# First layer's last block by halves: two head groups and the feed-forward in 256-token halves, two tiles per bank, seam transposes by DMA, a new table of settings

## The chip, the cores and the metric

One core of one Trainium2 chip runs the whole program. The metric is device time in microseconds (us) of one launch, lower is better. "The page" below is the page of one profiled execution; its span runs from that execution's first to its last instruction.

## What is computed

Two identical layers over 2048 tokens of width 512, each an attention with 32 heads of 16 and a gated feed-forward of width 1792, both with a layer norm ahead and a residual add behind. Inputs are bf16.

```python
def _A_ref(x, wqkv, wo):                      # H = 32, Dh = 16
    q, k, v = split(x @ wqkv)                 # (B, H, S, Dh) each
    p = softmax(einsum("bhqd,bhkd->bhqk", q, k) * Dh ** -0.5)
    return merge(einsum("bhqk,bhkd->bhqd", p, v)) @ wo
def _B_ref(x, w_gate, w_up, w_down):
    return (gelu(x @ w_gate) * (x @ w_up)) @ w_down
x = A_x
for _ in range(2):
    x = x + _A_ref(_layernorm(x), A_wqkv, A_wo)
    x = x + _B_ref(_layernorm(x), B_w_gate, B_w_up, B_w_down)
return x
```

## The kernel before

Everything stays on chip between the loads and the sixteen output stores. The order of all work is made at build time by a planner at the end of `_build`: it keeps a clock of its own per engine, looks at which pieces of work could start, and emits one at a time, so that each engine gets a fixed list of instructions with semaphore waits. The table `PLAN` gives the planner twenty numbers that change along the program (its key counts the first pass's score tiles planned so far, in fours); they say, among other things, how long a lead the first pass may have, from which lead a copy out of PSUM goes to VectorE and not to ScalarE, and how many small matmuls go at a time.

**Attention** is done per unit: four heads (a head group, eight groups per layer) by one block of query tokens (512; the second layer's last 512 are two blocks of 256). A unit goes through two passes.

- First pass: TensorE multiplies 128 queries by 512 keys of one head into one PSUM bank (L2453), VectorE takes the row maxima of one or two banks at a time (L2468) into PM. GpSimd joins the maxima (L1597 to L1602), VectorE transposes them (L1608), and SyncE's DMA queue writes the negative maximum into a spare row of QT (L1626).
- A tile can be folded: GpSimd subtracts two key blocks (KD, L2039), TensorE multiplies with the difference (L2276), ScalarE takes its relu (L2283), and one VectorE instruction (L2463, with a short read of its accumulator) adds it to the second tile's scores and takes the maximum. That spares VectorE one of two tiles and costs ScalarE one.
- Second pass: TensorE multiplies keys by queries (L2331), ScalarE takes the exponential of one or two banks (L2303) into a slot of SCR, and TensorE multiplies with V (L2356, 17 columns, the last for the sum) into bank 7. `nrm` divides (L1650 on ScalarE, L1656 and L1661 on GpSimd) into ATT.

**Behind a block's last unit** follow the output projection (ATT transposed into ATTT, matmul with WO, residual add into X at L1669 on VectorE, or L1674 on ScalarE and L1676 on GpSimd), a layer norm (statistics on VectorE or GpSimd, XN), its transpose into XNT, and the feed-forward `ffn`. In it a gate matmul fills a bank with one tile of the hidden width, the bank is copied to HT (L1309 VectorE, L1311 ScalarE), five instructions `gate` make the gelu on GpSimd (L1799, L1801, L1803, L1807, L1809) with a tanh on ScalarE (L1805), an up matmul fills another bank, and the product is taken either on VectorE straight from PSUM (L1971) or by a copy on ScalarE (L1977) and a multiplication on GpSimd (L1979). The down matmuls and the residual add close the block. The last block of a layer takes ScalarE's gelu (L1958) in place of `gate`; during it no exponentials are planned. Matmuls of projections and feed-forwards are L1294.

**Transposes** go one of two ways. `transpose_tile`: four 128x128 TensorE transposes into a bank (L1423) and one copy out (L1309, L1311). `transpose_dma`: one DMA transpose issued on SyncE's queue (L1430), SBUF to SBUF. Before the change the DMA way is taken for all blocks except the first layer's last one (its ATT, and XN both of its feed-forward and of the next layer's input), and except the program's end.

**The seam.** The second layer's attention needs keys of all 2048 tokens. So behind the last exponential of the first layer its last block has to run through projection, feed-forward, layer norm and key projection before the second layer's second pass can begin. The planner fills that time with first-pass tiles of six units on the keys that are there. TensorE also gets matmuls on zeros (L2486) where the planned load of the last microseconds is low.

`SPL` and `SPL0` are the numbers of last head groups that go by halves in the last block of the second and of the first layer; `half_of` and `u_half` mark these halves, and a halved block gets two output projections and two feed-forwards.

## Time and profile before

| what | us |
|---|---|
| median of 3 runs (lowest, highest) | 2467.43 (2465.78, 2468.37) |
| the profiled execution's own time | 2465.77 |
| its span | 2464.0 |
| busy in it: TensorE / VectorE / ScalarE / GpSimd | 2394.3 / 2393.6 / 2321.7 / 1271.1 |
| granted TensorE clock | 1.000 |

Busy time counts overlapping instructions of an engine once. The mean of a group counts each instruction from start to end, and neighbours overlap a little, so a mean is more than what an instruction adds to its engine. TensorE's busy time holds the matmuls on zeros.

### The profile page before, as it was taken

Reading aid. Unit: us, or ns where it says so; the run is one execution under the profiler, and the core shown is the slowest. Engines: PE = TensorE matmul, PEld = TensorE weight load, DVE = VectorE, ACT = ScalarE, POOL = GpSimd, SP = SyncE. Lnnn points to the kernel's source line nnn. Section 1 sums busy time; section 2 is a strip of 40 time slices with the busy share of each in tenths; the row PEclk is TensorE's granted clock in tenths of the full one; section 3 lists DMA queues with packets and bytes.
Section 4 is the critical chain, followed back from the end, with each engine's and each line's share of the span. In section 5 each row is a group of like instructions: output and inputs, shape, how many; then the busy total and the mean of one; then the engine's idle time right before and its main releaser. Section 6 shows DMA issues by size and latency. Waiting matters only on the chain.

```text
span 2464.0 us, 69105 instructions
## 1 busy us (share of the span) xinstructions
PE 2394.3 (97%) x29671; PEld 1141.9 (46%) x29671; DVE 2393.6 (97%) x3252; ACT 2321.7 (94%) x3103; POOL 1271.1 (52%) x2168
## 2 busy tenths in 40 slices
PE   8999999999999999999999999999999999999999
PEld 3444444444444444444433555454454444444456
DVE  9999999999999999999999999999999999999995
ACT  7999999999999999999966999999999999999897
POOL 5121137975579645965243211379317781279482
DMA  3110000000000001001000000000000000000000
GB/s 95 49 60 9 4 13 13 2 6 11 15 11 2 9 8 21 4 8 28 4 7 10 5 4 4 13 13 4 10 4 17 7 2 8 13 15 4 18 5 13
DMA packets 62747, 33.64 MB, mean 14 GB/s; under 512 B 44904, under 2 KB 61416, under 8 KB 62440
## 3 DMA queue, kind: packets, MB, share of 16 engines
q1 hardware_dynamic: 62440, 29.22, 4.8%
q8 instruction: 232, 3.80, 0.6%
q14 instruction: 75, 0.61, 0.1%
HBM read 9.70 MB, written 2.10 MB: 5 GB/s over the span
## 4 chain that ended last, share of the span: by engine, by line
DVE 38%; PE 36%; ACT 24%; POOL 1%; issue 1%; DMA 0%; POOLq 0%; ACTq 0%; DVEq 0%; SPq 0%
DVE PM L2468 34%; ACT SCR L2303 22%; PE PS L2453 12%; PE PS L1294 10%; PE PS L2356 8%; PE PS L2331 3%; PE PS L2486 2%; DVE SCR L2463 2%; ACT SCR L2283 1%; DVE HT L1971 1%; DVE HT L1092 0%; PE PS L2276 0%; ACT ACCS L1650 0%; ACT SCR L1805 0%; PE PS L1423 0%
## 5 line engine op out<-in xcount | busy, mean ns | idle before, releaser
L2468 DVE TENSOR_REDUCE PM<-PS 128x1 f32<-128x512 f32 (+1 forms) x2502 | 2162.7, 927 | 34.7 <-PE PS L2331 13.6
L2303 ACT ACTIVATE SCR<-PS 128x1024 bf16<-128x1024 f32 (+1 forms) x2439 | 2012.1, 929 | 67.8 <-PE PS L2331 48.7
L2453 PE MATMUL PS<-KT,QT 32*128 32x512 bf16 x3870 | 1027.3, 384 | 40.2 <-DVE PM L2468 23.2
L2331 PE MATMUL PS<-QT,KT 32*128 32x512 bf16 (+2 forms) x4864 | 920.5, 349 | 3.1 <-ACT SCR L2303 1.8
L2356 PE MATMUL PS<-VP,SCR 128*128 128x51 bf16 (+1 forms) x16384 | 812.3, 187 | 12.8 <-ACT SCR L2303 8.4
L2356 PEld LDWEIGHTS PS<-VP,SCR 128*128 128x128 bf16 x16384 | 576.3, 96 | 507.9 <-issue 426.6
L2453 PEld LDWEIGHTS PS<-KT,QT 32*128 32x128 bf16 x3870 | 245.1, 91 | 506.3 <-DVE PM L2468 301.7
L2486 PE MATMUL PS<-WV,ZER 128*128 128x240 bf16 x2031 | 377.8, 265 | 0.7 <-ACT SCR L2303 0.7
L1656 POOL TENSOR_TENSOR RL<-ACCS,CM 128x16 f32<-128x16 f32 (+2 forms) x66 | 179.6, 2721 | 359.1 <-ACT ACCS L1650 359.0
L2331 PEld LDWEIGHTS PS<-QT,KT 32*128 32x128 bf16 x4864 | 234.1, 91 | 68.8 <-ACT SCR L2303 41.7
L1597 POOL TENSOR_TENSOR PM<-PM 128x32 f32<-128x32 f32 (+2 forms) x76 | 18.5, 243 | 397.0 <-DVE PM L2468 385.7
L2486 PEld LDWEIGHTS PS<-WV,ZER 128*128 128x128 bf16 x2031 | 153.2, 96 | 51.5 <-issue 43.8
L2463 DVE CUSTOM_DVE_ANT_0 SCR<-PS,SCR 128x512 bf16<-128x512 f32 x226 | 145.8, 685 | 2.6 <-PE PS L2453 1.0
L1294 PE MATMUL PS<-WD,HT 128*128 128x512 bf16 x448 | 139.3, 381 | 0.4 <-DVE AO L2020 0.2
L1294 PE MATMUL PS<-XNT,WU 128*128 128x512 bf16 (+2 forms) x560 | 136.1, 338 | 2.3 <-DVE HT L1971 1.0
L2283 ACT ACTIVATE SCR<-PS 128x1024 bf16<-128x1024 f32 (+1 forms) x116 | 120.3, 1042 | 11.3 <-PE PS L2276 10.2
L1294 PE MATMUL PS<-XNT,WG 128*128 128x512 bf16 (+2 forms) x560 | 130.2, 338 | 0.7 <-ACT HT L1311 0.3
L2039 POOL TENSOR_TENSOR KD<-KT 128x512 bf16<-128x512 bf16 x74 | 85.4, 1154 | 86.8 <-PE PS L2276 76.2
L1799 POOL TENSOR_TENSOR SCR<-HT 128x512 bf16<-128x512 bf16 (+1 forms) x98 | 96.0, 980 | 43.0 <-ACT HT L1311 33.7
L1809 POOL TENSOR_TENSOR HT<-HT,SCR 128x512 bf16<-128x512 bf16 (+1 forms) x98 | 106.3, 1085 | 5.0
L1803 POOL TENSOR_TENSOR SCR<-SCR,HT 128x512 bf16<-128x512 bf16 (+1 forms) x98 | 106.2, 1085 | 2.4
L1676 POOL TENSOR_TENSOR X<-X,AO 128x512 f32<-128x512 f32 x42 | 53.2, 1268 | 75.4 <-ACT AO L1674 75.0
(128 smaller groups left out, 1498.3 us busy)
## 6 DMA issues: line engine op xcount, KB each, us to landing
KT<-SG SPq DMA_DIRECT2D x64, 64.0 KB
QT<-SG SPq DMA_DIRECT2D x56, 64.0 KB
QT<-MT SPq DMA_DIRECT2D x216, 1.0 KB
out_dram<-AO SPq DMA_DIRECT2D x16, 128.0 KB, 1.7
WG<-in_B_w_gate_dram SPq DMA_DIRECT2D x4, 448.0 KB, 4.8
WU<-in_B_w_up_dram SPq DMA_DIRECT2D x4, 448.0 KB, 4.9
WD<-in_B_w_down_dram SPq DMA_DIRECT2D x4, 384.0 KB, 4.6
QT<-MT SPq DMA_DIRECT2D x72, 0.5 KB
```

Source lines behind the costliest of these rows:

```text
L1294: ins = e.matmul(out_ap, lhsT=l, rhs=r_, start=(i == 0), stop=(i == n - 1))
L1656: emit("pool", lambda e: e.tensor_tensor(RL[:, s, 0:4 * nq], lsum, CM1[:, 0:4 * nq], op=ALU.pow), r=[("ACCS", s), ("CM1",)], w=[("RL", s)] ...
L1803: emit("pool", lambda e: e.tensor_tensor(u, u, ht, op=ALU.mult), r=ku + kh, w=ku, dur=0.18 + n / 520.0)
L1809: emit("pool", lambda e: e.tensor_tensor(ht, ht, u, op=ALU.mult), r=ku + kh, w=kh, dur=0.18 + n / 520.0)
L2283: emit("act", lambda e: e.activation(PT[:, s0:s0 + cnt, :], PS[:, bk:bk + cnt, :], ACTF.Relu), r=bks, w=[("PT", s0 + d) for d in range(cnt ...
L2303: emit("act", lambda e: e.activation(dst, src, ACTF.Exp, scale=DH ** -0.5), r=[BK[bk + i] for i in range(cnt)], w=[("PT", i) for i in slot ...
L2331: ins = e.matmul(bank(bk)[:, i * n:(i + 1) * n], lhsT=KT[32 * j:32 * j + 32, g, kt * 128:(kt + 1) * 128], rhs=QT[32 * j:32 * j + 32, s, c0 ...
L2356: ins = e.matmul(acc, lhsT=PT[:, slot, i * nh + (qt - q0) * 128:i * nh + (qt - q0 + 1) * 128], rhs=AP(VP, (kt * H + 4 * g + j) * 17, [[NTT ...
L2453: ins = e.matmul(bank(b), lhsT=QT[32 * j:32 * j + 32, s, qt * 128:(qt + 1) * 128], rhs=KT[32 * j:32 * j + 32, g, kb * 512:(kb + 1) * 512], ...
L2463: emit("dve", lambda e, i=i, b=b, sl=sl: e.tensor_tensor_reduce(PT[:, sl, :], bank(b), PT[:, sl, :], 1.0, -3.0e38, ALU.add, ALU.max, po[:, ...
L2468: emit("dve", lambda e: e.tensor_reduce(po, PS[:, bs[0]:bs[0] + cnt, :], axis=AX.X, op=ALU.max), r=bks, w=[("PM", sm) + h[1:] for h in hs] ...
L2486: return e.matmul(PS[:, b, NACC:512], lhsT=ZER[:, :], rhs=WV[:, 0, 0:512 - NACC], start=(b != 7), stop=(b != 7), skip_group_check=True)
```

## The change

Four switches of `_build` change, and the table is new: 566 entries in place of 625, 347 keys in common, one of these with the same numbers.

```diff
-... FAST=1, TG=1, ... SPL0=0, ... HQ=0, TP=1, LAGX=84, G2=0, CAL=0, XD=3, XDT=0.6, XDN=4):
+... FAST=1, TG=1, ... SPL0=2, ... HQ=0, TP=1, LAGX=84, G2=0, CAL=0, XD=15, XDT=0.6, XDN=2, PK=1):
...
-    0: (0.4, 0.35, 0.65, 0.32, 1.0, -0.05, 3, 1, 62, 84, 8, 80, 0.1, 1.5, 10, 10, 1, 4, 11, 84),
...
-                if XD & 1 and not fast and (tts[-1] < 12 or (tag[0] == "mid" and tag[1] == NL - 1)):
+                if XD & 1 and not fast and (XD & 4 or tts[-1] < 12 or (tag[0] == "mid" and tag[1] == NL - 1)):
...
-            dt = XD & 2 and not lastb and (la == NL - 1 or t0 + n < S)
+            dt = XD & 2 and not lastb and (XD & 8 or la == NL - 1 or t0 + n < S)
...
-        def gate(ft, n, due, done, cnt=1):
-            if cnt == 2:
+        def gate(ft, n, due, done, cnt=1, h=None, pk=False):
+            hc = (256 + h * n if h is not None and n <= 128 else h * n if h else 0) if HQ else n if h == 1 else 0
+            if cnt == 2 and not pk:
...
+                u = PT[:, sl, 0:cnt * n].rearrange("p (a b) -> p a b", a=cnt) if pk else PT[:, sl, 0:n]
...
             done = set()
-            for ft in range(NFT if tg else 0):
+            pk = PK and tg and n == 256
+
+            def gemm_p(W, wkey, f0, hk):
...
+                for i in range(2):
+                    if i:
+                        yield ("pe", [], [], NCK * n / 2300.0)
+                    pairs = [(W[:, ck, (f0 + i) * 128:(f0 + i + 1) * 128], XNT[:, ck, t0:t0 + n]) for ck in range(NCK)]
+                    emit_pe(mm_fn(bank(b)[:, i * n:(i + 1) * n], pairs, range(NCK)), NCK, n, r=xk + [(wkey,)], w=[BK[b]])
...
+            for f0 in range(0, NFT if pk else 0, 2):
+                hk = [k for ft in (f0, f0 + 1) for k in ht_keys(ft, h, n)]
+                b = yield from gemm_p(WG, "WG", f0, hk)
+                evac(HV[:, f0:f0 + 2, :], bank(b)[:, 0:2 * n].rearrange("p (a b) -> p a b", a=2), [BK[b]], hk, 2 * n)
+                add(gate(f0, n, due, done, 2, h, True), due)
+            for ft in range(NFT if tg and not pk else 0):
...
+            for f0 in range(0, NFT if pk else 0, 2):
...
+                yield ("cond", lambda f0=f0: f0 in done and f0 + 1 in done)
+                b = yield from gemm_p(WU, "WU", f0, hk)
...
+                if fast or pick() == "dve":
+                    emit("dve", lambda e, src=src, dst=dst: e.tensor_tensor(dst, src, dst, op=ALU.mult),
...
+                    emit("act", lambda e, b=b, o=o: e.activation(AO[:, o, 0:2 * n], bank(b)[:, 0:2 * n], ACTF.Copy),
...
+                    emit("pool", lambda e, dst=dst, o=o: e.tensor_tensor(
...
-            for ft in range(NFT):
+            for ft in range(0 if pk else NFT):
```

With `SPL0=2` the last two of the eight head groups of the first layer's last block are four units of 256 tokens in place of two of 512; the first half's output projection and feed-forward can go ahead of the second half's exponentials. `PK` puts two 256-token tiles of the hidden width into one bank, so that one copy, one gate and one product serve both; it holds for the first half here (the second half, as a layer's last, takes ScalarE's gelu, one tile at a time) and for the second layer's first 256-token block. Bits 4 and 8 of `XD` send the seam's transposes by DMA, twelve 128-token tiles in all. `XDN` is how many units of SyncE's issue time the planner books for a DMA transpose. The shorter table and the new code shift the line numbers: L2468 before is L2455 after, L1971 is L1952, L1977 is L1958, L1294 is L1235, L2331 is L2318, L2453 is L2440, L1430 is L1371.

Three places show how the instructions move. **TensorE around the last exponentials of the first layer.** Before, the last matmuls for exponentials (QT,KT) stand among products with V (VP,SCR) and first-pass tiles (KT,QT):

```order
L2453 MATMUL PS<-KT,QT 128x512 x2
L2331 MATMUL PS<-QT,KT 128x512 x2
L2356 MATMUL PS<-VP,SCR 128x3x17 x3
L2356 MATMUL PS<-VP,SCR 128x51
L2356 MATMUL PS<-VP,SCR 128x2x17
```

After, there are 256-token tiles, and the first half's gate matmuls (WG) stand between them, its first up matmuls (WU) right behind:

```order
L1235 MATMUL PS<-XNT,WG 128x256 x4
L2440 MATMUL PS<-KT,QT 128x512
L1235 MATMUL PS<-XNT,WG 128x256 x4
L2318 MATMUL PS<-QT,KT 128x256 x4
L2343 MATMUL PS<-VP,SCR 128x3x17 x4
L2440 MATMUL PS<-KT,QT 128x512 x2
L2343 MATMUL PS<-VP,SCR 128x3x17 x8
L1235 MATMUL PS<-XNT,WU 128x256 x8
```

All 56 gate matmuls of the first half now stand ahead of the last of those; before, all gate matmuls of that block stood behind.

**SyncE's queue over the seam.** QT<-SG and QT<-ZER fill queries, KT<-SG the keys, QT<-MT the negative maxima. Before:

```order
L1573 DMA QT<-ZER 4x4x128
L1575 DMA QT<-SG 64x512
L1489 DMA KT<-SG 64x512 x14
L1626 DMA QT<-MT 4x2x32 x8
L1626 DMA QT<-MT 4x4x32 x20
```

After:

```order
L1514 DMA QT<-ZER 4x4x128
L1516 DMA QT<-SG 64x512
L1371 DMA_TRANSPOSE ATTT<-ATT 128x4x128 x2
L1430 DMA KT<-SG 64x512 x6
L1371 DMA_TRANSPOSE XNT<-XN 128x4x128 x6
L1430 DMA KT<-SG 64x512 x8
L1567 DMA QT<-MT 4x2x32 x8
L1567 DMA QT<-MT 4x4x32 x20
```

Eight transposes now stand in that stretch of the queue, which had none, and the last eight key moves stand behind six of them.

**The product of the feed-forward in the first layer's third block.** Before, on VectorE, between the first-pass reductions:

```order
L1971 TENSOR_TENSOR HT<-PS,HT 128x512
L2468 TENSOR_REDUCE PM<-PS 128x1
L2468 TENSOR_REDUCE PM<-PS 128x2
L1608 STREAM_TRANSPOSE MT<-MSEL 128x32
L2468 TENSOR_REDUCE PM<-PS 128x1
L1971 TENSOR_TENSOR HT<-PS,HT 128x512
L2468 TENSOR_REDUCE PM<-PS 128x2
```

After, the same products are copies on ScalarE, between the exponentials (L2290), with a multiplication on GpSimd behind each:

```order
L2290 ACTIVATE SCR<-PS 128x1024
L2290 ACTIVATE SCR<-PS 128x512
L1958 ACTIVATE AO<-PS 128x512
L2290 ACTIVATE SCR<-PS 128x1024
L2290 ACTIVATE SCR<-PS 128x512
L1749 ACTIVATE SCR<-SCR 128x512
L1958 ACTIVATE AO<-PS 128x512
```

Over the first layer's first three blocks 25 of 42 products were on VectorE; now 3 are.

More of the change, by code (lines that the diff above doesn't have):

```diff
@@ L1947, in ffn @@
                 if not G2:
[L1948 removed]
+                    add(gate(ft, n, due, done, 1, h), due)
                 elif ft % 2:
[L1950 removed]
+                    add(gate(ft - 1, n, due, done, 2, h), due)
             if not tg:
```

41 lines of the change are left out of this document (31 added, 10 removed), and 1188 rows, old and new, of the table PLAN.

## The prediction

> **What bounds the kernel now.** First the page's busy times, the slices of the span and the chain of waits:
>
> ```profile
> PE 2394.3 (97%) x29671; PEld 1141.9 (46%) x29671; DVE 2393.6 (97%) x3252; ACT 2321.7 (94%) x3103; POOL 1271.1 (52%) x2168
> DVE  9999999999999999999999999999999999999995
> ACT  7999999999999999999966999999999999999897
> POOL 5121137975579645965243211379317781279482
> DVE 38%; PE 36%; ACT 24%; POOL 1%; issue 1%; DMA 0%; POOLq 0%; ACTq 0%; DVEq 0%; SPq 0%
> ```
>
> VectorE is idle for 2464.0 - 2393.6 = 70.4 us, ScalarE for 142.3. TensorE's 97% holds matmuls on zeros, so it is no bound over the whole span. ScalarE has its hole in slices 20 and 21: the seam. GpSimd is loaded in stretches, those of the feed-forwards. So I cut the span at the seam with the view of windows; the cuts are the last exponential of the first layer, the first of the second, and the 768th exponential bank after it (columns: length, then busy us of PE, weight loads, DVE, ACT, POOL):
>
> ```profile
> core 0: us, PE busy (x) PEld busy (x) DVE busy (x) ACT busy (x) POOL busy (x), PEclk, DMA share, GB/s
> 0.00:1224.50 1224.50, 1188.21 (x14405) 556.57 (x14405) 1208.83 (x1662) 1178.11 (x1564) 664.38 (x1165) 1.00 0.07 19
> 1224.50:1337.90 113.40, 108.77 (x596) 37.54 (x595) 107.41 (x195) 68.13 (x97) 49.29 (x100) 1.00 0.04 10
> 1337.90:1709.50 371.60, 365.05 (x5012) 185.65 (x5013) 359.99 (x459) 367.40 (x424) 144.22 (x244) 1.00 0.03 7
> 1709.50:2464.00 754.50, 732.25 (x9660) 362.15 (x9658) 717.40 (x939) 708.05 (x1019) 413.23 (x660) 1.00 0.04 10
> ```
>
> Four stages. **A**, 1224.5 us: VectorE idle 15.7, ScalarE 46.4; VectorE bounds. **B**, the seam, 113.4 us: VectorE idle 6.0, TensorE 4.6, ScalarE 45.3. **C1**, 371.6 us: ScalarE idle 4.2, VectorE 11.6; here ScalarE bounds, since VectorE came out of the seam with a lead. **C2**, 754.5 us: VectorE idle 37.1, ScalarE 46.4, much of it at the end. Shorter windows say how close the two engines can come:
>
> ```profile
> 0.00:44.00 44.00, 37.05 (x262) 18.87 (x262) 38.66 (x74) 33.08 (x51) 30.67 (x51) 1.00 0.44 132
> 44.00:88.00 44.00, 42.70 (x429) 16.73 (x429) 43.63 (x83) 38.42 (x56) 5.26 (x21) 1.00 0.05 13
> 440.00:484.00 44.00, 43.19 (x460) 17.95 (x456) 43.16 (x53) 41.64 (x66) 40.92 (x48) 1.00 0.01 2
> 880.00:924.00 44.00, 42.41 (x580) 21.63 (x575) 43.95 (x63) 43.96 (x50) 12.94 (x36) 1.00 0.03 5
> 2420.00:2464.00 44.00, 40.76 (x659) 28.41 (x659) 18.32 (x53) 28.50 (x56) 4.72 (x13) 1.00 0.06 17
> ```
>
> Where no feed-forward runs (880 to 924) both are full. In a feed-forward (440 to 484) ScalarE has 2.4 us free, VectorE 0.8, and GpSimd is 93% busy. ScalarE's 46.4 us in A are 16.5 at the start (10.9 and 5.6) and some 30 later. The last 44 us idle VectorE for 25.7; that tail has the same instructions after the change, but for two more exponential banks (40 for 38) behind the last first-pass tile, some 1 us.
>
> **Prices.** The group rows of the page give what neighbours overlap:
>
> ```profile
> L2468 DVE TENSOR_REDUCE PM<-PS 128x1 f32<-128x512 f32 (+1 forms) x2502 | 2162.7, 927 | 34.7 <-PE PS L2331 13.6
> L2303 ACT ACTIVATE SCR<-PS 128x1024 bf16<-128x1024 f32 (+1 forms) x2439 | 2012.1, 929 | 67.8 <-PE PS L2331 48.7
> ```
>
> 2502 x 0.927 is 2319.4 us, busy 2162.7: 0.063 us of each reduction lies over its neighbour. On ScalarE it is (2439 x 0.929 - 2012.1) / 2439 = 0.104. The forms apart, by lines:
>
> ```profile
> L2468 DVE TENSOR_REDUCE PM<-PS 128x2 f32<-128x1024 f32 x1142 | 1387.8, 1218 | 22.4 <-PE PS L2331 8.3 <-PE PS L2453 7.2 <-PE PS L2276 0.7
> L2468 DVE TENSOR_REDUCE PM<-PS 128x1 f32<-128x512 f32 x1360 | 914.2, 682 | 12.3 <-PE PS L2331 5.3 <-PE PS L2453 3.3 <-PE PS L2276 0.3
> L2463 DVE CUSTOM_DVE_ANT_0 SCR<-PS,SCR 128x512 bf16<-128x512 f32 x226 | 145.8, 685 | 2.6 <-PE PS L2453 1.0 <-PE PS L2331 0.7
> L2463 DVE DVE_READ_ACCUMULATOR2_ANT PM<- 128x1 f32 x226 | 18.8, 83 | 0.0
> L1971 DVE TENSOR_TENSOR HT<-PS,HT 128x512 bf16<-128x512 f32 x48 | 32.7, 681 | 0.2 <-PE PS L1294 0.2
> L2303 ACT ACTIVATE SCR<-PS 128x1024 bf16<-128x1024 f32 x1657 | 1607.5, 1079 | 52.9 <-PE PS L2331 38.0 <-DVE PM L2468 1.1 <-PE PS L2453 0.3
> L2303 ACT ACTIVATE SCR<-PS 128x512 bf16<-128x512 f32 x782 | 460.9, 611 | 14.9 <-PE PS L2331 10.6
> L2283 ACT ACTIVATE SCR<-PS 128x1024 bf16<-128x1024 f32 x110 | 116.5, 1065 | 11.3 <-PE PS L2276 10.2
> L1977 ACT ACTIVATE AO<-PS 128x512 f32<-128x512 f32 x50 | 30.5, 610 | 5.6 <-PE PS L1294 5.6
> ```
>
> Less the overlap: VectorE reduction of two banks 1.155, of one 0.619, fold 0.622 + 0.083 = 0.705, product 0.618; ScalarE exponential of two banks 0.975, of one 0.507, relu of two 0.961, copy 0.506.
>
> **The change part by part**, each engine's instructions counted in the order before and after and priced so.
>
> *Stage A.* VectorE: 22 products fewer (25 to 3), -13.6; 15 folds fewer, -10.6; 10 two-bank and 7 one-bank reductions more, +15.9; layer-norm statistics and transposes of the second half, +1.7. Sum -6.6. ScalarE: 22 copies for products more, +11.1; 16 one-bank exponentials more and 8 two-bank ones fewer, +0.3; relus 5 two-bank and 5 one-bank fewer, -7.4; some eleven copies and tanhs more, the first half's gate copies among them, +5.5. Sum +9.5. So VectorE would need 1202.2 and ScalarE 1187.6. If VectorE bounds as before, A shortens by 6.6, and ScalarE's idle time falls from 46.4 to 30.3, of which 16.5 are the start: 14 us left over 1130, closer than now but not closer than the window 880 to 924. The other end: ScalarE keeps its 46.4 idle us, and A grows by 9.5. The order keeps folding where VectorE would be late, so the two meet; I take -4.5, near the first end, since VectorE is the fuller engine in every feed-forward window. The two-tile copies and products (128x2x256) have no row; they lie between one copy of 512 (0.506) and two of 256, and I take the former, at most 3 us for all of them.
>
> *Stage B.* VectorE's list in it has 5 reductions, 2 statistics and one product fewer, 118.4 to 113.5 us by the same prices: -4.9. ScalarE -3.9. TensorE: 244 matmuls of 512 columns (two of 256 counted as one) for 280, because the first half's gate matmuls and half of the projection went ahead; no transposes for 12 groups of four; 24 matmuls on zeros more:
>
> ```profile
> 1323.27 2.76 PE L1294 MATMUL PS<-XNT,WK 128*128 128x512 bf16 x12
> 1333.65 0.79 PE L2486 MATMUL PS<-WV,ZER 128*128 128x240 bf16 x6
> 1320.96 0.34 PE PS L1423 x4
> 1321.32 0.61 ACT XNT L1311
> L1430 SPq DMA_TRANSPOSE XNT<-XN x38: 1188/1192/1935, 372.2 to 2339.8; - x38
> DMA to landing us min/median/max: 2.3/2.4/4.4
> ```
>
> Twelve in 2.76 us are 0.21 each: 36 x 0.215 = 7.7; the transposes' four in 0.34 add some 0.25 us, 12 x 0.25 = 3.0; zeros +24 x 0.1 = 2.4 (six in 0.79 are 0.1 each behind the first); with five first-pass tiles fewer in all -8.8. A transpose of one token tile takes 0.95 us by TensorE and ScalarE, and by DMA 1.2 us of SyncE's queue and 2.4 to landing, 3.6 together: 2.6 later per step. What hides it are the first-pass tiles, which TensorE's list has between every two steps. Both engines are 95% busy in B, so it shortens by between 4.9 and 8.8 if the chain holds, and by nothing or grows if it doesn't (below). I take -4.5.
>
> The Trainium skill (VectorE: DVE Perf Modes, "The three transpose paths" and "Rules for kernel authors") gives a 128x128 transpose 390 ns on TensorE and 1309 ns by DMA, and advises TensorE where a PSUM destination will do; the trace agrees in direction (0.95 for 3.6 with a tile of four). By that rule the seam is the fourth rival.
>
> *Stages C1 and C2.* C1: ScalarE 3.0 less, VectorE 6.5 more, of which its 11.6 idle us can hold all; between -3.0 and +2; I take -1. C2: VectorE -1.1, ScalarE +0.4 (66 one-bank exponentials more, 33 two-bank ones fewer, 10 copies for products moved); between -1.1 and +0.4; -0.5, and the tail's 1 us is in the range.
>
> *GpSimd.* 30 products of 512 elements more over the program, 22 of them in A, and seven gates of the first half, each of five instructions; by lines, and the instructions of one line:
>
> ```profile
> L1799 POOL TENSOR_TENSOR SCR<-HT 128x512 bf16<-128x512 bf16 x84 | 87.4, 1041 | 42.4 <-ACT HT L1311 33.2 <-DVE HT L1309 9.0
> L1801 POOL TENSOR_SCALAR SCR<-SCR 128x512 bf16<-128x512 bf16 x84 | 52.0, 620 | 6.7
> L1803 POOL TENSOR_TENSOR SCR<-SCR,HT 128x512 bf16<-128x512 bf16 x84 | 96.8, 1154 | 2.1
> L1979 POOL TENSOR_TENSOR HT<-HT,AO x60: 672/1162/1182, 473.2 to 2411.1; 128x512 bf16<-128x512 bf16 x50, 128x256 bf16<-128x256 bf16 x10
> ```
>
> A gate is 1.04 + 0.62 + 1.15 and once more the last two, 4.6 us; seven are 32 us ahead of the first half's up matmuls, for which 76 first-pass tiles stand from its first gate matmul to its last up matmul, 46 us of VectorE. The products are 22 x 1.16 = 25.5 us more in A. I cost both at nothing: GpSimd is busy 664.4 of 1224.5 us in A, 49.3 of 113.4 in B. In a feed-forward's 93% that cover is thin; gone, it costs the 25.5 us (fifth rival).
>
> The Trainium skill (Perfetto Trace Analysis, "Optimizing Scalar/DVE Operations") says that VectorE and GpSimd share a read port of SBUF, so that moving work between them might not help. The trace shows no such contention: GpSimd's products of 512 stay within 1182 ns at most while VectorE is 97% busy. If the rule held, the moved products would bring nothing, as in the third rival.
>
> **Sum.** -4.5 - 4.5 - 1.0 - 0.5 = -10.5 us on the profiled execution's 2465.8 (span 2464.0 and 1.8 around it), which lies 1.7 under the median; on the median 2467.4 - 10.5 = **2457** us.
>
> **The rivals.**
> 1. *The forecast*: 2452 to 2462.
> 2. *TensorE is what bounds the seam, and VectorE keeps its pace in A*: -6.6 - 8.8 - 3.0 - 1.1 = -19.5, 2448. For it: TensorE is idle least in B. Against: it needs every stage at its end.
> 3. *ScalarE becomes the bound in A*: the two engines share the loss, (-6.6 + 9.5) / 2 = +1.5, with B and C as taken -4.5, 2463. For it: 14 us of slack over 1130. Against: the window 880 to 924.
> 4. *The DMA transposes set the seam's chain*: three steps in series (ATTT, XNT, XNT), 3 x 2.6, and the second tile of each pair behind the first on the queue, 3 x 1.2, make 11.4 late; 6.0 of idle VectorE time take some of it, so B is -4.9 + 5.4 = +0.5 and the sum -5.5: 2462. For it: the last eight key moves are queued behind six transposes on SyncE, and the first exponential waits for them. Against: SyncE is free for most of B, and first-pass tiles stand between.
> 5. *GpSimd becomes the bound in the feed-forwards*: TensorE's list stands in order, so an up matmul that waits for a late gate holds the first-pass tiles behind it and so VectorE. Price 25.5 us in A in place of a gain: 25.5 - 6.6 - 4.5 - 1.5 = +13, 2480. It decides the sign from some 13 us not hidden. For it: 93% in those windows. Against: 45% idle over A, and TensorE's list can put a late product anywhere in a block's stretch.
>
> **How the numbers follow.** Chances: 0.47, 0.12, 0.14, 0.10, 0.17. What a measurement can tell from no change is about 0.2%, 4.9 us: faster is under 2462.5, slower over 2472.4. Faster: 0.46 of the forecast, 0.12, 0.04 of the third, 0.05 of the fourth: 0.67. Slower: the fifth and 0.01 of the third: 0.18. Same: 0.15. Prices and the settings' own shifts, a quarter of the 36 us that VectorE idles outside start and tail, widen the forecast's ends by some 5; the range 2446 to 2471 holds the second to fourth and leaves the fifth out.
>
> **What would show it.** In the profile after: products on VectorE 15, folds 207, VectorE busy 2393.6 - 6.1 = 2387 or so, ScalarE about 3 more; the last exponential of the first layer near 1220; the hole between exponentials near 109 us with VectorE still 95% busy in it. A hole over 113 us, with TensorE waiting for DMA XNT or for GpSimd's HT, proves me wrong in B; ScalarE full in A's windows while VectorE idles proves the third; TensorE's up matmuls waiting for GpSimd HT the fifth.

## The result, and the profile after

| what | before | after |
|---|---|---|
| median of the runs, us (lowest, highest; count) | 2467.82 (2465.78, 2470.03; 6) | 2455.56 (2454.78, 2459.94; 6) |
| ratio, 95% interval | | 0.9955 (0.9942 to 0.9968) |
| the profiled execution's own time / its span | 2465.77 / 2464.0 | 2458.00 / 2456.3 |

The change makes the kernel 12.3 us faster at the median; the forecast was 2457. From the page of the changed kernel, busy times and the chain of waits by engine:

```profile
PE 2363.2 (96%) x29657; PEld 1152.1 (47%) x29900; DVE 2388.4 (97%) x3217; ACT 2321.6 (95%) x3154; POOL 1332.0 (54%) x2207
PE 40%; DVE 39%; ACT 19%; issue 1%; POOL 1%; POOLq 0%; ACTq 0%; DVEq 0%
```

VectorE is busy 5.2 us less, ScalarE as long as before, GpSimd 61 us more. The groups of both engines, forms apart:

```profile
L2455 DVE TENSOR_REDUCE PM<-PS 128x2 f32<-128x1024 f32 x1151 | 1396.8, 1216 | 23.2 <-PE PS L2318 8.3 <-PE PS L2440 6.7 <-PE PS L2263 0.4
L2455 DVE TENSOR_REDUCE PM<-PS 128x1 f32<-128x512 f32 x1380 | 925.0, 680 | 8.7 <-PE PS L2318 3.7 <-PE PS L2440 1.6
L2450 DVE CUSTOM_DVE_ANT_0 SCR<-PS,SCR 128x512 bf16<-128x512 f32 x207 | 132.7, 684 | 3.0 <-PE PS L2440 0.9 <-PE PS L2263 0.5 <-PE PS L2318 0.3
L1952 DVE TENSOR_TENSOR HT<-PS,HT 128x512 bf16<-128x512 f32 x15 | 10.2, 680 | 0.0
```

```profile
L2290 ACT ACTIVATE SCR<-PS 128x1024 bf16<-128x1024 f32 x1613 | 1565.4, 1081 | 54.7 <-PE PS L2318 43.7 <-DVE PM L2450 0.2
L2290 ACT ACTIVATE SCR<-PS 128x512 bf16<-128x512 f32 x870 | 507.9, 616 | 12.6 <-PE PS L2318 7.8
L1958 ACT ACTIVATE AO<-PS 128x512 f32<-128x512 f32 x69 | 42.8, 621 | 0.5 <-PE PS L1235 0.4
```

The instructions are those of the sum: 15 products and 207 folds on VectorE, and the mean of each form on VectorE stays within 2 ns of its row before. Only ScalarE's +3 us are missing.

**The stages.** Here my reading of before had a slip. This is ScalarE's timeline of the kernel before around the cut that I called the last exponential of the first layer (start, length, engine and line, what):

```profile
1212.42 6.69 ACT L2303 ACTIVATE SCR<-PS 128x1024 bf16<-128x1024 f32 x7
1219.78 1.02 ACT L2283 ACTIVATE SCR<-PS 128x1024 bf16<-128x1024 f32 x1 [0.67 <-PE PS L2276]
...
1223.43 1.02 ACT L2283 ACTIVATE SCR<-PS 128x1024 bf16<-128x1024 f32 x1
```

The exponentials are L2303 and end at 1219.1. What ends at 1224.45 is a relu of a fold, L2283: same tiles, same shape, another line. So stage A of before was cut 5.4 us too late. The prediction's counts of instructions were taken from the order, with the right cut; its own list for B tells the two apart, 118.4 us of VectorE in a stage of 113.4. The windows of before with the right cut (length, then busy us of PE, weight loads, DVE, ACT, POOL, then the granted clock):

```profile
0.00:1219.10 1219.10, 1182.85 (x14372) 555.03 (x14372) 1203.65 (x1652) 1173.86 (x1558) 661.13 (x1163) 1.00 0.07 19
1219.10:1338.00 118.90, 114.12 (x629) 39.07 (x628) 112.68 (x206) 72.39 (x105) 52.55 (x101) 1.00 0.04 10
1338.00:1710.10 372.10, 365.64 (x5016) 185.74 (x5016) 360.49 (x459) 367.99 (x426) 144.79 (x245) 1.00 0.03 7
1710.10:2464.00 753.90, 731.65 (x9658) 362.06 (x9655) 716.80 (x939) 707.45 (x1018) 412.65 (x660) 1.00 0.04 10
```

The first profile after ran its seam at half clock for a while (below), so the same four stages are shown of a second profile of the changed kernel, whose seam has a clock of 1.00 (the second repeat):

```profile
0.00:1219.60 1219.60, 1171.53 (x14428) 561.53 (x14552) 1200.98 (x1624) 1180.99 (x1592) 709.53 (x1217) 1.00 0.07 19
1219.60:1329.90 110.30, 104.07 (x645) 42.96 (x651) 105.73 (x195) 67.75 (x105) 63.58 (x121) 1.00 0.09 20
1329.90:1703.40 373.50, 365.14 (x5046) 187.60 (x5061) 367.68 (x472) 366.42 (x422) 138.01 (x237) 1.00 0.03 7
1703.40:2454.40 751.00, 722.01 (x9549) 360.23 (x9638) 714.75 (x929) 706.57 (x1038) 420.66 (x634) 1.00 0.04 10
```

A +0.5, B -8.6, C1 +1.4, C2 -2.9: -9.6 of span. A cut tells when ScalarE reaches a point, not how much work of VectorE, the engine that bounds most of the span, lies behind it. So I also counted in both traces (sums over the rows of these lines) when VectorE has taken the n-th of its 4096 first-pass banks, a fold counting as two, and when ScalarE has taken the n-th of 4096 exponential banks; 2048 of each is a layer:

| bank | VectorE before | first profile after | second repeat | ScalarE before | first profile after | second repeat |
|---|---|---|---|---|---|---|
| 512 | 295.8 | -0.8 | +0.4 | 338.8 | -1.4 | -0.2 |
| 1024 | 591.1 | -5.0 | -3.7 | 633.0 | -3.9 | -2.7 |
| 1536 | 882.3 | -3.4 | -3.0 | 924.5 | -4.2 | -3.7 |
| 1920 | 1107.5 | -6.0 | -5.5 | 1153.9 | -8.3 | -7.9 |
| 2048 | 1180.7 | -3.8 | -3.3 | 1219.1 | 0.0 | +0.5 |
| 2560 | 1466.5 | -3.4 | -5.4 | 1576.7 | +1.2 | -0.7 |
| 3584 | 2100.7 | -4.1 | -6.0 | 2137.5 | -4.0 | -5.9 |
| 4096 | 2423.7 | -9.8 | -11.6 | 2440.9 | -8.0 | -9.9 |

The second repeat starts some 1 us behind the first profile (half clock near 24 us) and leaves the seam 2 us ahead of it. Three gains are to be explained: 4 us in the first layer, which vanish at its last exponential and come back in the seam; little in C1; and 5 to 6 us in the last blocks.

### The profile page after: what moved, and what is told of

It is laid out like the page before. It is cut to its first block, busy times and chain, and to the rows that moved or that the text cites. A ratio compares the mean times of both kernels' runs of the same rounds, so it can differ in the third digit from the quotient of the medians.

```text
span 2456.3 us, 69380 instructions
## 1 busy us (share of the span) xinstructions
PE 2363.2 (96%) x29657; PEld 1152.1 (47%) x29900; DVE 2388.4 (97%) x3217; ACT 2321.6 (95%) x3154; POOL 1332.0 (54%) x2207
## 4 chain that ended last, share of the span: by engine, by line
PE 40%; DVE 39%; ACT 19%; issue 1%; POOL 1%; POOLq 0%; ACTq 0%; DVEq 0%
DVE PM L2455 35%; ACT SCR L2290 17%; PE PS L2440 14%; PE PS L2343 10%; PE PS L1235 9%; PE PS L2318 4%; PE PS L2473 3%; DVE SCR L2450 2%; ACT SCR L2270 1%; DVE HT L1033 0%; PE PS L2263 0%; ACT HT L1252 0%; ACT SCR L1749 0%; DVE AO L2001 0%; DVE HT L1952 0%
## 5 line engine op out<-in xcount | busy, mean ns | idle before, releaser
L2455 DVE TENSOR_REDUCE PM<-PS 128x2 f32<-128x1024 f32 (+1 forms) x2531 | 2182.1, 924 | 31.9 <-PE PS L2318 12.0
L2290 ACT ACTIVATE SCR<-PS 128x1024 bf16<-128x1024 f32 (+1 forms) x2483 | 2014.1, 918 | 67.3 <-PE PS L2318 51.5
L2440 PE MATMUL PS<-KT,QT 32*128 32x512 bf16 x3889 | 1034.6, 385 | 47.2 <-DVE PM L2455 28.8
L2318 PE MATMUL PS<-QT,KT 32*128 32x512 bf16 (+2 forms) x4992 | 921.4, 344 | 2.1 <-ACT SCR L2290 1.3
L2440 PEld LDWEIGHTS PS<-KT,QT 32*128 32x128 bf16 x3889 | 246.5, 91 | 512.1 <-DVE PM L2455 304.6
L2473 PE MATMUL PS<-WV,ZER 128*128 128x240 bf16 x2064 | 389.8, 267 | 1.8 <-ACT SCR L2290 0.9
L2318 PEld LDWEIGHTS PS<-QT,KT 32*128 32x128 bf16 x4992 | 236.7, 91 | 58.4 <-ACT SCR L2290 28.0
L2450 DVE CUSTOM_DVE_ANT_0 SCR<-PS,SCR 128x512 bf16<-128x512 f32 x207 | 132.7, 684 | 3.0 <-PE PS L2440 0.9
L2270 ACT ACTIVATE SCR<-PS 128x1024 bf16<-128x1024 f32 (+1 forms) x104 | 110.4, 1063 | 14.5 <-PE PS L2263 12.3
L1235 PE MATMUL PS<-XNT,WU 128*128 128x512 bf16 (+2 forms) x553 | 118.7, 316 | 5.0 <-issue 2.4
L1235 PE MATMUL PS<-XNT,WG 128*128 128x512 bf16 (+2 forms) x565 | 118.5, 317 | 4.7 <-issue 2.7
L1743 POOL TENSOR_TENSOR SCR<-HT 128x512 bf16<-128x512 bf16 x98 | 101.8, 1039 | 38.8 <-ACT HT L1252 31.4
L1235 PE MATMUL PS<-WD,HT 128*128 128x512 bf16 x387 | 118.4, 381 | 4.1 <-issue 2.2
L1753 POOL TENSOR_TENSOR HT<-HT,SCR 128x512 bf16<-128x512 bf16 x98 | 112.9, 1153 | 4.5
L1747 POOL TENSOR_TENSOR SCR<-SCR,HT 128x512 bf16<-128x512 bf16 x98 | 112.8, 1152 | 1.5
```

The source lines that it names most:

```text
L1235: ins = e.matmul(out_ap, lhsT=l, rhs=r_, start=(i == 0), stop=(i == n - 1))
L1747: emit("pool", lambda e: e.tensor_tensor(u, u, ht, op=ALU.mult), r=ku + kh, w=ku, dur=0.18 + n / 520.0)
L1753: emit("pool", lambda e: e.tensor_tensor(ht, ht, u, op=ALU.mult), r=ku + kh, w=kh, dur=0.18 + n / 520.0)
L2270: emit("act", lambda e: e.activation(PT[:, s0:s0 + cnt, :], PS[:, bk:bk + cnt, :], ACTF.Relu), r=bks, w=[("PT", s0 + d) for d in range(cnt ...
L2290: emit("act", lambda e: e.activation(dst, src, ACTF.Exp, scale=DH ** -0.5), r=[BK[bk + i] for i in range(cnt)], w=[("PT", i) for i in slot ...
L2318: ins = e.matmul(bank(bk)[:, i * n:(i + 1) * n], lhsT=KT[32 * j:32 * j + 32, g, kt * 128:(kt + 1) * 128], rhs=QT[32 * j:32 * j + 32, s, c0 ...
```

## The experiments

Most switches cannot be undone alone: the planner then lays out everything behind them anew, with a table made for another state. So five kernels below (experiments 2, 3, 6 and 7) keep the changed kernel's order: the planner books the same costs as in the changed kernel, and either another instruction is issued in a place (`ghost` books without issuing), or matmuls on zeros are added or left out. Times of runs are medians (lowest, highest), each beside runs of the kernel before on the same chip.

**1. The changed kernel again** (no edit), with a second profile.

> The changed kernel once more, for a second profile. Theory: what its first profile lost at the seam's end was the TensorE clock of that one execution (granted 0.50 to 0.87 between 1324 and 1336 us), not the order of the work. At a clock of 1.00 throughout, the first exponential of the second layer starts near 1328.5 us, 3 us ahead of the 1331.6 of the first profile, and the span is near 2453. Rival: the order itself is slow there; then the first exponential starts near 1331.6 again with the clock at 1.00, and the 3 us lie elsewhere.

Median 2460.18 (2455.55, 2466.02), ratio 0.9972 (0.9963 to 0.9981). The profile has the half clock in the same place again. Windows of 4 us over the seam's end (PEclk is the third number from the right):

```profile
1318.00:1322.00 4.00, 3.27 (x23) 1.63 (x22) 4.00 (x4) 2.48 (x3) 0.00 (x0) 1.00 0.34 87
1322.00:1326.00 4.00, 2.92 (x21) 1.33 (x18) 4.00 (x6) 0.00 (x0) 1.36 (x6) 0.96 0.00 0
1326.00:1330.00 4.00, 4.00 (x14) 1.13 (x14) 2.68 (x4) 0.00 (x0) 1.32 (x6) 0.50 0.00 0
1330.00:1334.00 4.00, 3.83 (x28) 2.03 (x27) 2.81 (x6) 1.78 (x2) 0.00 (x0) 0.69 0.01 3
```

The second repeat (experiment 6), with the same load in the first two of these windows and full clock:

```profile
1318.00:1322.00 4.00, 3.27 (x21) 1.40 (x20) 4.00 (x4) 2.48 (x3) 0.00 (x0) 1.00 0.41 102
1322.00:1326.00 4.00, 2.92 (x23) 1.57 (x21) 4.00 (x5) 0.00 (x0) 1.36 (x6) 1.00 0.00 0
```

Clock lost in experiment 1: 4 x (0.04 + 0.50 + 0.31) = 3.4 us, that is 6.8 us at half clock. Ahead of it TensorE waits for VectorE (busy 2.92 of 4 us); under it VectorE starves (2.68 of 4). The first exponential of the second layer starts at 1332.2. This run alone settles neither theory: that the half clock sits in the same place twice (and a third time in the profile of experiment 7's repeat) says that it belongs to the order, and the second repeat shows an execution of the same order without it, where the exponential starts at 1329.9, 2.3 us earlier. So the theory was right on the loss, and wrong in calling it that of one execution.

**2. Products back on VectorE**, order kept.

```diff
+                    if la == 0 and ft < 8:
+                        hk = ht_keys(ft, h, n)
+                        sch.op("dve", lambda e, bu=bu, ft=ft: e.tensor_tensor(HV[:, ft, :], bank(bu)[:, 0:n],
+                                                                              HV[:, ft, :], op=ALU.mult), r=[BK[bu]] + hk, w=hk)
+                        ghost("act", [BK[bu]], [("AO", o)], 0.055 + n / 1200.0)
+                        ghost("pool", [("AO", o)] + hk, hk, 0.18 + n / 520.0)
+                        continue
```

> 24 products of the first layer's first three blocks, whose copies the change has on ScalarE and whose multiplications on GpSimd, are taken on VectorE; every other instruction keeps its place. Theory of the prediction (VectorE bounds stage A, 0.618 us a product): VectorE needs 24 x 0.618 = 14.8 us more, and the last exponential of the first layer, near 1219 us in both kernels, comes 10 to 15 us later; the whole is 10 to 15 us slower. Rival one (VectorE waits for something else in the feed-forwards): the last exponential within 2 us of 1219, the whole within 3 us. Rival two (ScalarE bounds there, as in the prediction's third case): faster, by up to 24 x 0.506 = 12 us.

Median 2473.30 (2471.97, 2481.63), ratio 1.0032 (1.0021 to 1.0043). By lowest runs, both at a clock of 1.000, 16.4 us slower than experiment 1, over the 10 to 15 expected; by the two spans 14.4. The rows show that the edit also caught eight products of 256 in the seam:

```profile
L1971 DVE TENSOR_TENSOR HT<-PS,HT 128x512 bf16<-128x512 f32 x24 | 16.6, 690 | 0.0
...
L1971 DVE TENSOR_TENSOR HT<-PS,HT 128x256 bf16<-128x256 f32 x8 | 3.3, 417 | 0.0
```

Window up to the last exponential of the first layer:

```profile
0.00:1232.20 1232.20, 1175.23 (x14428) 560.42 (x14552) 1213.39 (x1648) 1172.62 (x1568) 683.33 (x1193) 1.00 0.07 19
```

The last exponential comes at 1232.2 for 1219.3, 12.9 us later for 14.8 us of added work; the banks show it in three steps, one per block: VectorE's 896th bank 4.0 late, the 1408th 9.9, the 1792nd 12.8. The profiled execution has half clock from 790 to 797 us, so part of the second step can be the clock's. So VectorE bounds stage A, and a product there moves the last exponential by some 0.54 us (12.9 / 24), nearly its price. ScalarE is 8 us less busy and gains nothing: both rivals fall.

**3. The seam's transposes by TensorE**, order kept: each of the twelve DMA transposes becomes four TensorE transposes and a copy on ScalarE.

```diff
+            if seam:
+                ghost("sp", list(rkeys), list(wkeys), XDT, grp, XDN)
+                b = take_bank()
...
+                        ins = e.transpose(bankbf(b)[:, ck * 128:(ck + 1) * 128], src_fn[:, ck * 128:(ck + 1) * 128], IDN[:, :])
...
+                sch.op("pe", pe_fn, r=list(rkeys) + [("IDN",)], w=[BK[b]])
+                sch.op("act", lambda e: e.activation(dst_fn, bankbf(b)[:, 0:NCK * 128].rearrange("p (a b) -> p a b", a=NCK), ACTF.Copy),
+                       r=[BK[b]], w=list(wkeys))
+                return
```

> The twelve transposes of the seam by TensorE, with the copies on ScalarE; every other instruction keeps its place. Theory of the prediction (DMA's longer way is hidden, TensorE and VectorE are full): from the last exponential of the first layer to the first of the second, 12 x 0.25 = 3 us longer at most, since TensorE gets that work back; between 0 and +3. Rival (the DMA transposes set the seam's chain, the prediction's fourth case): 5 us shorter or more, and the whole faster by as much. Second rival: the copies on ScalarE, in order behind other waits there, delay the chain: over 3 us longer.

Median 2472.46 (2466.34, 2481.51), ratio 1.0028 (1.0015 to 1.0040); by lowest runs 10.8 us slower than experiment 1. The second rival came true. Between the exponentials lie 121.4 us, 112.9 in experiment 1, and the last exponential itself comes 5.3 us later, since four of the twelve transposes stand ahead of it. TensorE's waits for the copies alone (L1395) add up to 6.1 us. Its waits from 1150 to the first exponential (lines here: L1391 transposes, L1395 their copies, L1246 projection and feed-forward, L2468 first pass, L2298 relu):

```profile
PE PS L1246 <- ACT XNT L1395: 2.6, 3, 1.6
PE PS L2468 <- DVE PM L2483: 2.5, 6, 0.7
PE PS L1391 <- ACT SCR L2298: 1.1, 3, 0.5
PE PS L2501 <- ACT XNT L1395: 1.0, 1, 1.0
...
PE PS L1246 <- ACT ATTT L1395: 1.0, 1, 1.0
```

In the changed kernel (second repeat) the same stretch has no wait for a transpose:

```profile
PE PS L2440 <- DVE PM L2455: 3.5, 9, 0.7
PE PS L1235 <- ACT AO L1940: 0.7, 2, 0.4
```

A transpose in TensorE's list waits there for the layer norm, for a bank that ScalarE has to clear, and its user for a copy that stands behind relus on ScalarE; the first-pass tiles behind it wait as well, and VectorE with them. On SyncE's queue nothing stands behind the wait but other moves.

**4. The seam's transposes by TensorE, planned so**: the switch alone, `XD=3` for 15.

> Bits 4 and 8 of the transposes' switch off: the planner lays the seam's transposes on TensorE, with the changed kernel's table; the order is the same up to about 1180 us. Read up to the first exponential of the second layer alone (behind it the order follows settings made for another state). Theory of the prediction (DMA's longer way is hidden and spares TensorE 3 us): the first exponential 0 to 3 us later than in the changed kernel, where it starts near 1329 at full clock. Rival one (the transposes by TensorE cost some 10 us, as in the kernel that kept the order): 8 us later or more. Rival two (the DMA way sets the chain): over 2 us earlier.

Median 2466.96 (2465.92, 2471.48), ratio 1.0003 (0.9994 to 1.0012). Windows up to the first exponential of the second layer:

```profile
0.00:1225.70 1225.70, 1176.81 (x14482) 564.49 (x14605) 1206.37 (x1632) 1186.49 (x1601) 716.13 (x1226) 1.00 0.07 19
1225.70:1337.30 111.60, 105.16 (x628) 41.16 (x638) 109.04 (x185) 62.06 (x102) 58.02 (x108) 1.00 0.04 11
```

The first exponential comes 7.4 us later than in the changed kernel (1337.3 for 1329.9), outside the 0 to 3 expected and nearly the first rival's 8. VectorE has taken 2348 first-pass banks by then and not 2340, but it is late too: its 2336th bank comes 3.6 us later, its 2348th 3.2. So the transposes cost between some 3 us, counted by VectorE's work, and 7.4, counted by the first exponential, and the run does not settle which counts: by the 2640th bank VectorE is 10.2 us late, and by lowest runs the whole is 10.4 us slower, but there the order follows settings made for another state. TensorE waits 0.2 us for a transpose's bank here and never for a copy of one: where the planner knows of the transposes it puts them where they wait little. Had the DMA way set the chain, both experiments would have brought the first exponential earlier; both brought it later.

**5. The second layer's 256-token block without pairs** (two tiles per bank).

```diff
-            pk = PK and tg and n == 256
+            pk = PK and tg and n == 256 and la == 0
```

> The second layer's first block of 256 tokens goes without two tiles per bank; the same settings, and the same order up to about 2250 us. Theory of the prediction (two tiles per bank are worth at most 3 us there, C2 moves by -0.5): 0 to 3 us slower. Rival: the gain that VectorE shows late (its 3840th first-pass bank comes 5.1 us earlier than before the change, its 3968th 11.3) is made by the pairs: 5 us slower or more. Second rival: it is made by the settings alone: within 1 us.

Median 2467.03 (2462.97, 2473.61), ratio 0.9999 (0.9991 to 1.0008); by lowest runs 7.4 us slower than experiment 1. The first rival came true in size, though not in the place it named: VectorE's last banks are as early as with pairs (the 3968th at 2335.1, 2.0 behind experiment 1, as are its banks since the seam), but the last exponential bank is 5.6 behind, the end 9.7. ScalarE's rows of that feed-forward, from 2300 us on, without pairs:

```profile
L1749 ACT ACTIVATE SCR<-SCR 128x256 bf16<-128x256 bf16 x14 | 6.0, 430 | 0.0
L1252 ACT ACTIVATE HT<-PS 128x256 bf16<-128x256 f32 x14 | 5.6, 401 | 1.2 <-PE PS L1235 1.1
L1958 ACT ACTIVATE AO<-PS 128x256 f32<-128x256 f32 x8 | 3.8, 472 | 0.7 <-PE PS L1235 0.7
```

and in the changed kernel (second repeat):

```profile
L1749 ACT ACTIVATE SCR<-SCR 128x512 bf16<-128x512 bf16 x7 | 4.5, 643 | 0.1
L1252 ACT ACTIVATE HT<-PS 128x512 bf16<-128x512 f32 x7 | 4.2, 604 | 0.0
L1940 ACT ACTIVATE AO<-PS 128x512 f32<-128x512 f32 x4 | 2.4, 606 | 0.0
```

15.4 us for 11.1: an instruction of 512 costs 0.60 to 0.64 us, two of 256 cost 0.80 to 0.94. These instructions run between 2349 and 2413 us; behind them ScalarE has the remaining exponentials to take, while VectorE runs out of first-pass work. The window from 2420 to 2440 us, without pairs and with them (second repeat):

```profile
2420.00:2440.00 20.00, 19.27 (x346) 11.07 (x352) 2.67 (x7) 19.89 (x23) 1.60 (x3) 1.00 0.08 22
2420.00:2440.00 20.00, 19.43 (x354) 15.12 (x357) 9.42 (x30) 16.46 (x33) 1.39 (x3) 1.00 0.06 16
```

ScalarE is full there without pairs, so its 4.3 us more make the last exponential late. The rest of the 7.4 is not taken apart; the settings behind the edit were made for a block with pairs, so 7.4 may be too much for the pairs alone.

**6. Fill the waits with matmuls on zeros**, order kept: 39 of them at the five places where TensorE's busy share over 3.4 us, counted in the trace, is lowest behind the start.

```diff
+        FILL = {3938: 6, 5720: 5, 7542: 2, 7547: 4, 7633: 6, 7652: 3, 7653: 6, 12080: 2, 12085: 2, 12088: 3}
...
+            for _ in range(FILL.get(pe_n[0], 0) if est(w=[BK[7]]) <= clk["pe"] else 0):
+                sch.op("pe", lambda e: e.matmul(PS[:, 7, NACC:512], lhsT=ZER[:, :], rhs=WV[:, 0, 0:512 - NACC], start=False, stop=False,
+                                                skip_group_check=True), r=[("ZER",), ("WV",)], w=[BK[7]])
+            pe_n[0] += 1
```

> The changed kernel with 39 more matmuls on zeros, in TensorE's waits at five places where its busy share over 3.4 us is lowest (0.68 to 0.78: near 649, 942, 1289, 1321 and 2021 us); every other instruction keeps its place. Theory: the spread of the changed kernel's runs (2455.6 to 2466.0 us at granted clocks from 1.000 down to 0.994) is stretches of 6.8 us at half clock that low load draws; with the places filled the median is 2455.5 to 2458, the highest run under 2462, and the profile shows no half clock near 1326. Rival one: the half clock does not hang on these places; median near 2460 and a spread as before. Rival two: the added matmuls cost time themselves; the fastest run is over 2458.

> The changed kernel once more, beside the runs of this call. Theory: its runs with a clock of 1.000 take 2455 to 2456 us, and each 0.001 to 0.0015 of mean clock lost adds 2 to 3.5 us; median between 2455 and 2461. Rival: runs of one clock differ by more than 2 us among themselves.

Filled 2457.11 (2455.29, 2460.72), ratio 0.9962 (0.9948 to 0.9976); the changed kernel beside it 2456.17 (2455.55, 2462.09), ratio 0.9959 (0.9947 to 0.9972). Both profiles have full clock in the seam. Five runs each tell the two apart in nothing: inconclusive, but the zeros cost no time that shows. One filled run still took 2460.72 us, at a clock of 0.998. The four repeats at 0.999 and 1.000 stay within 0.7 us, and the one at 0.996 takes 6 us more.

**7. Fill the start too, and empty the seam.** The first kernel has 19 more zeros in the waits between 18 and 23 us (`FILL` with 102: 3, 108: 8, 115: 8). The second goes the other way:

```diff
+            if not (("ZER",) in r and 7580 < pe_n[0] <= 7662):
                 sch.op("pe", fn, r=r, w=w)
```

> The changed kernel, as the measure for the other two runs of this call. Theory: runs at a clock of 1.000 take 2455 to 2456 us; the others 2 to 3.5 us more for each stretch of half clock; median between 2455 and 2461.

> As the kernel with 39 more matmuls on zeros, with 19 more of them in TensorE's waits between 18 and 23 us, where its busy share over 3.4 us is 0.39 in all kernels. Theory: half clock is drawn by low load at these places; so it shows less often than in the changed kernel beside it, the median is 1 us or more under that one's, and the highest run under 2460. Rival: both have the same median within 1 us and the same spread; then the half clock comes at other places, or not from the load within a few us.

> The changed kernel without the 46 matmuls on zeros that it issues between about 1305 and 1324 us; every other instruction keeps its place. Theory (low load draws the half clock): the profile shows half clock near the seam's end, for 6.8 us or longer, nearly every run has it, and the median is 3 us or more over the changed kernel's beside it. Rival (it comes by chance, whatever the load): median within 1.5 us of the changed kernel's.

> The kernel with 58 more matmuls on zeros once more, on whatever chip comes. Theory (low load at the filled places drew the half clock): again all runs at a clock of 0.999 or 1.000, median 2455 to 2457, highest under 2460. Rival (the even runs came from that chip): a spread up to 2460 and over, as the changed kernel showed on another chip (2455.6 to 2466.0).

On one chip: the changed kernel 2455.04 (2454.98, 2457.91), ratio 0.9954 (0.9940 to 0.9968); filled 2455.70 (2455.48, 2456.38), 0.9956 (0.9944 to 0.9969); emptied 2461.67 (2460.07, 2468.56), 0.9985 (0.9976 to 0.9994). On another chip the filled one 2455.78 (2455.38, 2456.09), 0.9955 (0.9941 to 0.9968). Two windows of the emptied kernel:

```profile
1306.00:1310.00 4.00, 1.86 (x10) 0.41 (x10) 3.97 (x10) 1.80 (x2) 2.07 (x10) 0.78 0.17 33
1310.00:1314.00 4.00, 4.00 (x13) 0.72 (x12) 3.16 (x10) 2.28 (x3) 0.00 (x0) 0.50 0.17 33
```

and two of the filled one, over the place of experiment 1:

```profile
1322.00:1326.00 4.00, 3.95 (x29) 2.10 (x28) 4.00 (x6) 0.00 (x0) 1.37 (x6) 1.00 0.00 0
1326.00:1330.00 4.00, 3.93 (x32) 1.88 (x32) 3.76 (x7) 0.59 (x1) 1.34 (x6) 1.00 0.01 0
```

All eleven runs of the emptied kernel have a mean clock of 0.996 or less and lie 5 us and more over the changed kernel's median; all ten of the filled one have 0.999 or 1.000. So low load draws the half clock here: the emptied kernel shows it on one chip. In all four sets of runs the changed kernel's 27 runs lie between 2454.78 and 2466.02, half of them over 2456.2, the filled kernel's ten between 2455.38 and 2456.38. At full clock filling gains nothing (about 0.5 us lost). That it takes away the long runs is likely and not shown: the chip on which the changed kernel had most of them (experiment 1) never ran the filled one, and on the chip that ran both the changed kernel has one run of five at 0.998. The median 1 us under the changed kernel's, as expected there, did not come: it is 0.7 us over.

**8. The last block without halves**: the switch alone, `SPL0=0` for 2.

> The first layer's last two head groups in one block again, without halves; the order is the same up to about 1080 us, with the changed kernel's table. Read up to the first exponential of the second layer alone. Theory: the halves move feed-forward work ahead of the last exponential and fill VectorE with it, so without them the last exponential comes earlier (1211 to 1217 us for 1219), the hole behind it is as long as before the change (117 to 121 us), and the first exponential of the second layer is 3 to 9 us later than in the changed kernel (1332 to 1338). Rival: the halves bring nothing; the first exponential within 2 us of the changed kernel's 1329, and the gain there is all of the products moved off VectorE.

Median 2504.07 (2499.53, 2506.53), ratio 1.0147 (1.0133 to 1.0161). Everything expected of it failed. The last exponential comes at 1236.3, the first of the second layer at 1363.4, and VectorE's banks leave the changed kernel's already from the 1700th on, 4.5 us late near 976 us: the order differs from about 940 us on, not from 1080, and this execution has half clock from 962 to 972 us. With this table the planner needs the halves; that is not what the halves are worth. Their share stays open: with either table alone it can't be had.

## Why the prediction was right, and where it was not

**The sum.** Forecast -10.5 us. The lowest runs on one chip (experiment 1), both at full clock, are 2466.19 before and 2455.55 after: -10.6. The medians of the first runs give -12.3. That the sum fits so closely is partly luck. Up to the end of C1 the forecast had -10.0 and the windows show 0.5 - 8.6 + 1.4 = -6.7; C2 brought -2.9 where it had -0.5. Two misses of 3.3 and 2.4 us nearly cancel.

**Stages A and B, -4.5 each.** The step that failed is the cut "the last exponential": it was a relu, 5.4 us behind it. With the right cut A is +0.5 and B -8.6, together -8.1 for -9.0. What A was to gain is there (VectorE has finished the first layer's first pass 3.8 us earlier in the first profile, forecast -4.5), but not at that cut: the last two head groups, now by halves, take 1219.6 - 1146.1 = 73.5 us from the 1920th exponential bank on, before 1219.1 - 1153.9 = 65.2:

```profile
1153.90:1219.10 65.20, 63.69 (x851) 32.11 (x851) 64.78 (x79) 64.41 (x80) 11.00 (x15) 1.00 0.04 11
1146.10:1219.60 73.50, 71.23 (x1027) 37.98 (x1033) 70.98 (x88) 71.31 (x107) 35.23 (x48) 1.00 0.10 24
```

ScalarE, 97% busy there, has 6.9 us more to do: the exponentials by halves take 67.1 us for 63.2 (42 of one bank for 15), and six gate copies and three tanhs 5.6. TensorE, with the gate matmuls between, is as full, so which of the two sets the length is open. I had counted those instructions and not asked when they would be paid. They shorten the hole behind.

VectorE's work fell less than summed: its busy time by 2.7 us in A (forecast 6.6) and by 7.0 in B (forecast 4.9), 9.6 for 11.5 together. One term is mis-sized by a double count: the short read of a fold starts inside the fold, as in these rows of before, so that a fold adds 0.61 us (600.51 to 601.12) and not 0.705, 1.4 us for the 15 folds of A:

```profile
600.51 0.68 DVE L2463 CUSTOM_DVE_ANT_0 SCR<-PS,SCR 128x512 bf16<-128x512 f32 x1
601.12 0.08 DVE L2463 DVE_READ_ACCUMULATOR2_ANT PM<- 128x1 f32 x1
601.12 0.69 DVE L2463 CUSTOM_DVE_ANT_0 SCR<-PS,SCR 128x512 bf16<-128x512 f32 x1
```

**The price of a product**, 0.618 us of VectorE, held: some 0.54 at the last exponential (experiment 2). VectorE bounds A, ScalarE had the room: its busy time in A went up 7.1 us, forecast 9.5. The third rival falls, and no slowdown of GpSimd by VectorE shows either: its products of 512 have a median of 1160 ns and a maximum of 1172 (before 1162 and 1182), with 30 more of them.

```profile
L1960 POOL TENSOR_TENSOR HT<-HT,AO x83: 667/1160/1172, 467.4 to 2289.5; 128x512 bf16<-128x512 bf16 x69, 128x256 bf16<-128x256 bf16 x14
```

**B, between -4.9 and -8.8 "if the chain holds".** The chain held; B lies at the far end, with VectorE busy 105.7 of 110.3 us, 96%. But the changed kernel leaves the seam with 2340 first-pass banks taken for 2348: of the 8.1 us that A and B gain together, 8 banks at 1.216 / 2, that is 4.9 us, are work left for later. Five of these banks are B's (229 taken in it for 234), the other three were missing at its start. C1 pays for it: VectorE's idle time there falls from 11.6 to 5.8 us, ScalarE's rises from 4.1 to 7.1, and C1 is +1.4 where I had -1.0.

**The DMA transposes**, taken as hidden: right, TensorE has no wait for one in the seam. What they spare, priced at 3.0 us, is between 3 and 7.4 at the first exponential where the planner lays them on TensorE (experiment 4), and 10.8 of the whole where the order is kept (experiment 3). The fourth rival falls: without them the first exponential comes later. The advice of the Trainium skill (VectorE: DVE Perf Modes, "Rules for kernel authors") to use TensorE where PSUM will do is about one transpose; the runs here speak against it in this seam, where a wait in TensorE's list is what costs.

**C2, -0.5**: measured -2.9. The mis-sized term is "at most 3 us for all" pairs: the one block in the second layer is worth up to 7.4 (experiment 5), 4.3 of ScalarE's busy time by rows. I had priced pairs only as neither dearer nor cheaper than a copy of 512, and left out that they replace two of 256. That is in C2 alone; ScalarE's missing +3 lie elsewhere for the most part: its busy time by stages is 3.1 us under the forecast in A and B together, 1.4 over it in C1 and 1.3 under it in C2. VectorE's gain late in C2 is not the pairs': from its 3840th to its 3968th bank it takes 78.5 us, before 84.6, and 78.4 without pairs; three products and two statistics less on it there are 3.4 of the 6.1. From the last first-pass bank to the end the kernel takes 2454.4 - 2412.0 = 42.4 us, before 40.3: the tail costs 2.1, forecast 1. What else moved within C2 isn't taken apart.

**GpSimd as the bound**, the fifth rival, falls. TensorE's waits over the whole span of the changed kernel:

```profile
PE PS L2440 <- DVE PM L2455: 28.8, 116, 1.6
PE PS L1235 <- issue: 10.0, 63, 0.2
PE PS L2343 <- ACT SCR L2290: 7.9, 34, 0.5
```

GpSimd is not among the twelve longest, whose last is 0.6 us. The second rival, every stage at its end, fails by C1.

**Not in the prediction at all**: the clock. I read 1.00 in every window of before and took it as given. The new order has places of lower load: counted over 3.4 us and away from start and end, TensorE's busy share falls to 0.68 near 1321 us in all four profiles, in the kernel before nowhere under 0.77. Beside the experiments 9 of 21 runs of the changed kernel have a mean clock of 0.998 or less, of the kernel before 3 of 68. In its first two profiles that costs 1.7 and 2.3 us up to the first exponential of the second layer, in the worst run some 10.

## What to carry to other kernels

A stage is cut at an instruction's line, not at its tile and shape, and progress is compared by the work that the bounding engine has done: a cut on another engine moves when work is shifted across it. What a DMA transpose saved here was less TensorE's time than a wait in a list with other work behind it (experiment 3); how much that counts depends on where the planner would have put it, and experiment 4 leaves that open. Ahead of a change in the order, look for the stretches where TensorE is least busy over some 3.4 us (half of the 6.8 us that the half clock lasted), and behind it compare the spread of the runs, not only their median.

## What the runs showed of the hardware

TensorE's clock fell to half where TensorE had been busy 3.27 and 2.92 us of two windows of 4, its longest wait in them 0.7 us, in some executions and not in others (in three of four profiles of the changed kernel, not in the second repeat). In the emptied kernel, where a window has 1.86 of 4, the profile shows it and every run has a mean clock of 0.996 or less. The loss adds up to 6.8 us at half clock in experiment 1, and to 4 x (0.22 + 0.50) = 2.9 us of clock in the two windows shown of the emptied kernel alone. The Trainium skill (TensorE: Matmul & The Clock Gate, "Part 1: The HAM clock gate") has a window of 3413 ns that runs free of the kernel and throttles after an idle one: 6.8 us is two such windows, and a free-running window would explain why one order shows it in some runs only. That it takes an idle window does not agree with the rows: TensorE was busy for 0.68 of the emptiest 3.4 us there.

The runs price it: in experiment 1 a mean clock of 0.994 goes with 2466.02 us and one of 1.000 with 2455.55, 1.7 us for each 0.001.

A pass over two tiles in one instruction saved ScalarE 0.2 to 0.3 us each time: a copy or tanh of 128x512 took 0.60 to 0.64 us, one of 128x256 0.40 to 0.47 (experiment 5).
